# A gated long convolution and a gMLP on one core: the short convolution done with tokens on partitions, its product regrouped inside SBUF

## The chip, the cores and the metric

The kernel runs on one core of a Trainium2 chip. The metric is the device time of one execution in microseconds (us). A core has five engines that run their own instruction lists side by side: TensorE (PE; its weight loads are shown as PEld), VectorE (DVE), ScalarE (ACT), GpSimd (POOL) and SyncE (SP), which here issues nearly all DMA transfers. SBUF is the working memory of 128 partitions, PSUM takes the results of matmuls.

## The reference

There are 2048 tokens of 640 channels. Part A is a short convolution over four tokens, a product with v, a long convolution over all earlier tokens, and a product with the modulated input; part B is a gated MLP whose gate mixes tokens. In short:

```python
mod = silu(c) @ w_mod                       # sa, ca, ga, sb, cb, gb
h = layernorm(x) * (1 + ca) + sa            # x is A_q
k_shift[s] = sum over t of k_pad[s + t] * shift_k[:, 3 - t]
kv = k_shift * v
y = irfft(rfft(kv, 2S) * rfft(ssm_k, 2S))[:S] + kv * ssm_D
x = x + ga * (h * y)
h = layernorm(x) * (1 + cb) + sb
z = gelu(h @ w_in); z1, z2 = halves of z; z2 = layernorm(z2)
out = x + gb * ((z1 * (w_sp @ z2 + b_sp)) @ w_out)
```

## The kernel before

The 640 channels are cut into five tiles of 128 (`u` or `dt` from 0 to 4). The long convolution is a transform by matmuls: a stage one (`stage1`, with the table `F1bd`), a second stage (`forward`, with the table `M2`, 8 items of two frequencies blocks each per tile), the product of the two spectra on VectorE (`product`, L462, tiles `T` or `Tf` with an optional sum `W` on GpSimd or VectorE), the inverse stage (`inv`, table `G2`, result `Z`), a transposing DMA (`zt`, L685) and the last stage (`y`). It is done for the filter (`XK`, `k_item`) and for the signal (`XU`, `u_item`).

Stage one wants the signal in a regrouped form: partition `(g n)`, with `g` one of 8 channels in a group and `n` one of 16 blocks of 128 tokens; along the free axis 16 channel groups `c` by 128 tokens `f` of the block. `ssm_k` is loaded so from DRAM by a rearranged access pattern (`load_X`, L390).

The signal comes from the short convolution. `load_kv` loads k and v of a channel tile by transposing DMAs (L521), so that channels lie on partitions and tokens along the free axis; tile 0 in two halves. `short_conv` makes four diagonal 128x128 matrices `dg` from the four taps. For each of four chunks of 512 tokens, `taps` runs four matmuls with `dg` stationary and k moving, shifted by 0 to 3 tokens, summed in a PSUM tile `sm`; `times_v` (L553) multiplies by v in place. A DMA then writes the product to a DRAM scratch `kv_scr` (`kvw`, L559), and `load_X` reads it back regrouped.

Beside this run the loads of `xt`, the layer norm statistics (`ln1`), the modulation rows from `w_mod` (`wm`), the gating (`gh`), the residual and, as soon as tokens are done, the gMLP: `zz` matmuls with `w_in` (tile `big`) into `pu` and `pz`, gelu on ScalarE, statistics (`stz`) and normalizing on VectorE; then the token mixing by `w_sp` and the output projection, which are written out in program order after the plan (L1013, L1137).

All operations up to the first mixing products are put into a `Plan`: each has the engines that may do it, its reads and writes. A long string `ORDER` gives the order in which they are issued and the engine of each (P, A, D, G, S). Each engine runs its list in that order; SP too, so a DMA whose wait is not yet met holds those behind it. Tiles rotate through a fixed number of buffers by tag, in `SLOTS`. All matmuls of the plan pass through a helper at L245, and copies through one at L248.

Of the kernel before, what the change touches and what calls it, by code (L numbers as in the profile page):

```python
# [10 lines left out]
ALU = mybir.AluOpType  # L11
# [4 lines left out]
P = 128  # L16
# [19 lines left out]
SLOTS = dict(Tf=2, W=2, X=3, X1=4, KH=9, T=3, Z=3, ZT=1, wm=1, big=2, dg=2, st1=2, s1=1, sm=2, pu=2, pz=2)  # L36
# [4 lines left out]
D0 D13 D100 G101 S88 A1 P1032 P7 A4 A10 G5 A23 D15 D102 D109 D103 D110 A112 D115 A111 S2 D6 P1033 P8 A11 D14 A16 D116  # L41
A117 A118 D104 A105 S19 P1034 P26 A106 D90 D121 S82 D86 D17 D122 D18 G119 G113 P1035 P145 A146 P148 D149 S21 S83 D87
P24 A124 A147 D27 D127 S20 A150 P227 A228 A114 P151 A123 A152 P154 A156 P28 D25 S22 A153 D29 D155 P233 A234 G125 A126
P30 S523 D31 D527 P139 D140 G120 S34 P161 A162 P163 S32 G107 P133 P229 G48 A164 S33 P169 A170 D134 D36 S3 P167 A168
A230 G108 P136 D137 P171 A172 P165 A166 P142 A143 G135 D528 P41 A128 D529 D530 D138 P157 A158 P159 A160 S35 G141 P231
A232 D42 S84 S85 P37 D38 P173 P176 A174 A175 D177 P43 D44 A178 P182 D183 P9 A12 G130 P179 A184 P39 D181 D40 A180 P185
D186 S524 A531 A532 P195 D196 P191 D192 S46 S47 P55 D56 A533 P247 A248 G187 G188 P189 S45 P211 D212 G197 G144 G198 P51
D52 A534 P201 D202 D535 P49 D50 G213 P205 G214 A190 S526 A542 P53 D206 P203 A204 G72 S89 P217 D218 G131 A543 P193 P221
D222 P251 A252 D194 P215 A216 A544 G536 D537 P235 P253 P199 D254 D54 A236 P241 A242 G60 S565 P566 G553 P257 A258 S525
D538 D539 S91 G207 G208 P237 P568 A238 P239 A240 P255 A256 G223 P245 D93 A246 P249 A250 S57 G549 G224 D554 G555 P225  # L50
A226 D200 P301 P259 D260 P291 D292 G556 P209 A302 P219 G261 G262 D540 S570 P303 A569 P269 A567 G550 G551 G552 D270
G271 P275 A304 A220 P573 D574 P307 A210 P571 D276 D572 G651 A308 P285 D286 D541 A545 P263 P293 S58 A294 P305 A306 P65
D614 P243 A264 P265 G707 D266 A244 D546 S92 P325 S59 D66 D672 G272 D593 A326 P63 D64 P315 A316 P327 D649 P273 G287
A328 P321 A322 D591 P267 A268 G288 P329 A330 S575 G547 D548 S70 P295 D296 D297 P578 D579 A274 P576 G561 D577 D562 D594
P313 A557 A314 P309 P331 A332 P61 D652 S94 D96 G298 D563 D564 G655 A310 P67 D62 P311 P375 D68 A312 P349 D350 P333 D334
P289 G597 D670 P73 A376 A558 A559 A560 P343 D344 P77 G598 P377 P317 A318 D129 A290 P277 A278 G335 D595 D596 A378 D653
G336 P323 A324 P299 D592 P337 A300 P319 A320 A338 G345 S71 D78 S599 G346 D74 D616 P379 A380 P369 G713 P600 G612 S69
P351 A352 P279 P347 D370 D601 P381 A382 P602 D280 D603 P365 P79 D366 D80 A348 G654 P604 P383 A384 S95 P399 A400 D605
P387 A388 P359 G281 G282 P283 A284 G371 G372 P401 A402 D360 P606 D607 G613 P353 D354 S97 P385 A386 D99 S580 D618 P403
A404 P75 P397 A398 P395 A396 D619 D671 P405 A406 P373 A374 P339 G361 G362 P363 A364 D615 P449 A450 G608 D76 P413 P367  # L60
A368 G355 D340 D414 P407 D408 P341 A342 G617 P453 G709 S620 P621 D622 G674 P393 D650 A454 P389 A394 A390 S81 G356 P623
D624 P451 A452 P439 D440 P357 A358 P625 D626 P391 A392 P455 P427 G409 G410 P627 P417 G609 P581 G673 G656 D428 G429
D430 A456 S98 P411 A412 D418 P471 A472 P473 D628 A474 D634 P431 P457 G419 G420 P443 P479 A458 D444 A480 D629 D632 P467
A468 P421 A432 P423 D424 G445 P475 A476 P433 D434 A582 S657 G639 A422 P415 G676 P461 A462 D631 P477 A478 D630 D638
P463 A464 P658 D659 A416 P465 A466 P441 A442 G446 P660 D635 P481 G435 P447 A448 P497 G710 D661 P662 G436 P437 A438
P425 A426 D482 D663 P664 D498 S583 P517 D518 G677 G483 G484 P485 A486 P507 D508 P499 P459 A460 P469 P501 A470 D665
G675 G519 G520 P521 A522 G509 G510 A500 A132 G708 P487 P584 D502 P513 D488 P511 A512 P491 P489 G503 A490 D514 P515
G504 D492 S678 G668 P505 P679 A516 A506 G493 D494 P495 A585 D633 D680 P681 D682 A496 P719 A720 D636 S586 P683 D684
P715 P721 A722 D716 P685 D686 D687 P717 A718 P587 A588 P723 P726 P725 G666 D691 G711 D689 D688 P724 D727 G714 G692
D728 D729 D758 D730 D759 G760 D690 D731 D732 D734 P735 P1037 D772 P1036 D761 A762 P749 D736 D750 D737 P589 S756 D741  # L70
D740 G763 P764 D766 D767 D768 S757 A590 G667 G610 D696 P765 A769 P742 D733 D738 D693 D834 D771 A770 D637 P794 G773
D695 D836 P812 P784 A795 A813 D751 D754 D774 P818 D837 P791 A775 D739 D694 D835 G697 D698 D776 P778 G838 A819 D839
A785 A840 D842 G843 P777 A782 A783 P787 A788 P816 A817 D780 G712 D841 P814 A815 D640 A792 D779 D781 P808 A809 D796
D752 P822 A823 S844 P820 A821 P824 A825 A846 P798 A848 D743 D789 D702 G669 D703 D706 G845 D744 D745 D746 D900 P801
D611 A799 D644 S1038 P805 A806 D793 P826 A802 A827 D641 D699 D901 D847 G849 P850 A851 D797 P857 P867 A868 D747 P892
A893 D643 D701 D755 D748 P882 D903 S1039 A883 D700 D642 D902 A858 P874 A875 D647 P880 G904 D905 D906 G908 D786 D907
D909 S910 D810 A881 P890 A891 P860 G915 A861 P864 A865 G911 P871 A872 P884 D1054 D1055 D1057 D705 D968 A912 D1056 D807
D811 G913 A885 D648 D704 D753 D645 D966 D646 D967 D969 G970 D866 P888 A889 S1040 D859 D862 D863 P886 A914 P878 A887
A879 P853 D790 D971 D972 G975 D973 A974 A854 D855 D800 P926 P916 A927 S1045 P937 A917 D852 D869 S976 D1046 D803 D804
P933 D918 S1041 A934 P930 P940 A938 D1048 A941 D876 D873 D877 D870 D856 D928 A931 D932 D980 P919 D942 A920 G894 P923  # L80
D921 A924 P948 P958 G979 P952 D895 A959 D922 A949 P946 P954 D977 A896 D925 D929 A947 A953 A955 D939 G978 G981 P982
A983 G828 P999 D1058 D1059 A897 D898 A1000 D943 P985 A986 P989 A990 P992 D829 D830 D831 D1049 A832 D833 D935 D936
D1001 D984 D987 A993 D988 P944 P1006 A945 A1007 P996 A997 D1062 P1003 A1004 D991 P956 G960 D961 D965 A962 A957 D1008
D998 D1002 D1005 D1009 P1020 S1043 A1021 A963 S1042 D994 D995 D899 D1063 P1012 P1014 A1013 P950 G1026 D1027 A1031 A951
D964 D1064 D1066 D1030 A1028 A1015 D1029 D1065 P1024 P1070 A1025 P1072 S1044 P1077 D1067 P1081 D1053 A1073 D1068 D1069
A1071 P1074 D1078 D1082 P1076 D1075 D1079 S1080 P1083 P1018 A1019 P1022 P1010 A1023 D1084 S1085 A1011 D1060 D1061
P1016 A1017 D1047 D1051 D1052 D1050
# [42 lines left out]
def kernel(  # L130
# [43 lines left out]
    dram = ctx.enter_context(tc.tile_pool(name="dram", bufs=1, space=bass.MemoryType.DRAM))  # L174
# [36 lines left out]
    with ExitStack() as pctx:  # L211
# [296 lines left out]
        kv_scr = dram.tile([D, S], BF16)  # L508
        kv_fft = kv_scr.rearrange("(c g) (n f) -> (g n) c f", g=8, f=P)
        SCH = 512  # L510

        def load_kv(dt):
            name = "kv%d" % dt

            n = 2 if dt == 0 else 1

            def load(e, v, h):
                if not v and h == 0:
                    new(name, "big", [P, 2 * S])
                src, o, m = (A_v if v else A_k), v * S, S // n  # L520
                e.dma_start_transpose(tl[name][:, o + h * m:o + (h + 1) * m], src[0, h * m:(h + 1) * m, dt * P:(dt + 1) * P])  # L521
            for v in range(2):
                for h in range(n):
                    ks = [("v", i) if v else ("k", i) for i in range(4 * h // n, 4 * (h + 1) // n)]
                    first = not v and h == 0
                    op("S", "ldk", lambda e, v=v, h=h: load(e, v, h), r=[] if first else [(name, "new")],
                       w=[(name, x) for x in ks] + ([(name, "new")] if first else []), new=[(name, "big")] if first else [], n=n)

        def short_conv(dt):
            name, dg = "kv%d" % dt, "dg%d" % dt  # L530
# [10 lines left out]
            for i in range(S // SCH):  # L541
                ps = "tp%d_%d" % (dt, i)

                def taps(e, i=i, ps=ps):
                    p_ = new(ps, "sm", [P, SCH], F32)
                    for j in range(4):
                        lo = 0 if i else j
                        mm(p_[:, lo:], tl[dg][:, j, :], tl[name][:, i * SCH - j + lo:(i + 1) * SCH - j], j == 0, j == 3)

# [661 lines left out]
```

## Time and profile before

| what | value |
|---|---|
| median of 3 runs | 310.95 us (309.45 to 311.83) |
| the profiled execution | 312.19 us, its span 310.4 us |
| granted TensorE clock | 0.999 |
| busy, share of the span | PE 95%, DVE 82%, ACT 52%, POOL 37% |
| DMA packets | 127953, 45.22 MB |
| queue q1 (hardware) | 68.3% of 16 engines' span |
| HBM | 16.11 MB read, 5.24 MB written |

The span is the time from the first to the last instruction in the profile. A row of a group gives the instructions of one kind, their total busy time and the mean of one in nanoseconds, then the idle time of that engine just before them and what ended it. DMA rows give the number of issues, their size and the median time from issue to landing. In the windows, each engine's busy time in a stretch stands with the number of its instructions, then the granted clock, the DMA share and GB/s. A timeline row gives start and length, both in us. Busy times of matmuls include their passage through the array, so four in a row take less than four times one.

### The profile page before, as it was taken

To read this page: it belongs to the slowest core of one execution; us is meant where nothing else is said; L and a number is where in the kernel's file an instruction comes from. 1 tells how busy PE (TensorE), PEld (TensorE's weight loads), DVE (VectorE), ACT (ScalarE), POOL (GpSimd) and SP (SyncE) were. 2 spreads that over 40 slices of the span, in tenths; PEclk is the share of its full clock that TensorE was granted. 3 is DMA by queue.
4 is the path that set the end of the run, shared out by engine and by line. 5 is a ranking of instruction groups with operands and counts; after the bars stand their busy time and mean duration, and the time that the engine had idled before them with its cause. 6 is when DMAs were issued, how large, how long until landed. Compare 5 with 4: busy or idle time off the path is not lost.

```text
span 310.4 us, 6397 instructions
## 1 busy us (share of the span) xinstructions
PE 295.9 (95%) x2499; PEld 197.3 (64%) x2506; DVE 254.1 (82%) x515; ACT 160.9 (52%) x288; POOL 116.0 (37%) x148
## 2 busy tenths in 40 slices
PE   7897989989999998989999999999999999999996
PEld 2575778867889998645555555455565656555564
DVE  8798998979998988999895998977676858567474
ACT  6987899978888957447666687140101010010100
POOL 2531878838988999555414612000000000000000
PEclk9999999999999999999999999999999999999999
DMA  8999999998995849405698930073938284840414
GB/s 170 216 227 217 257 310 226 207 203 191 221 226 121 193 95 295 143 2 98 123 159 208 185 36 0 2 123 76 201 82 190 63 176 108 131 102 0 104 30 114
DMA packets 127953, 45.22 MB, mean 146 GB/s; under 512 B 117071, under 2 KB 127156, under 8 KB 127924
## 3 DMA queue, kind: packets, MB, share of 16 engines
q1 hardware_dynamic: 127770, 44.78, 68.3%
q8 instruction: 19, 0.31, 0.4%
q14 instruction: 10, 0.08, 0.1%
q10 hardware_dynamic: 154, 0.05, 0.1%
HBM read 16.11 MB, written 5.24 MB: 69 GB/s over the span
## 4 chain that ended last, share of the span: by engine, by line
PE 37%; DVE 19%; POOL 2%; DMA 2%; issue 1%; ACT 1%; POOLq 1%; DVEq 0%; SPq 0%
PE ps L1013 23%; PE po L1137 10%; DVE stz L926 4%; DVE st L704 3%; DMA Z<-Z 2%; PE pz L1013 1%; DVE Tf L462 1%; PE pu L245 1%; DVE xt L698 1%; DVE X L943 1%; POOL rstd L191 1%; DVE T L998 1%; DVE T L462 1%; DVE mv L829 1%; DVE gh L746 1%
## 5 line engine op out<-in xcount | busy, mean ns | idle before, releaser
L245 PEld LDWEIGHTS <-Z 128*128 128x128 bf16 x320 | 31.2, 98 | 28.0 <-DVE Z L871 1.3
L245 PE MATMUL pu<-X,M 128*128 128x128 bf16 (+1 forms) x480 | 45.7, 237 | 2.5 <-DVE Tf L462 2.1
L245 PEld LDWEIGHTS <-M 128*128 128x128 bf16 x480 | 37.3, 98 | 8.7 <-issue 3.1
L1019 ACT COPY m<-ps 128x432 f32<-128x432 f32 x7 | 3.6, 518 | 72.7 <-PE ps L1013 72.7
L1013 PEld LDWEIGHTS <-S 128*128 128x128 bf16 x256 | 25.0, 98 | 22.9 <-issue 1.3
L476 POOL TENSOR_TENSOR W<-Tf 128x256 bf16<-128x256 f32 x47 | 34.7, 760 | 11.4 <-DVE Tf L462 8.1
L245 PE MATMUL pz<-big,Z 128*128 128x432 bf16 x160 | 33.1, 346 | 0.8 <-DVE Z L871 0.8
L248 ACT CAST X<-s 128x1024 bf16<-128x1024 f32 x31 | 31.9, 1030 | 3.1 <-PE s L245 2.9
L1137 PE MATMUL po<-w_o,uT 128*128 128x320 bf16 (+2 forms) x231 | 32.7, 295 | 0.0
L245 PE MATMUL pu<-big,Z 128*128 128x432 bf16 x160 | 32.5, 346 | 0.0
L462 DVE TENSOR_TENSOR Tf<-pu,KH 128x1024 f32<-128x1024 f32 x25 | 30.3, 1219 | 2.6 <-POOL gh L608 1.1
L1013 PEld LDWEIGHTS <-wT 128*128 128x128 bf16 x192 | 18.7, 98 | 15.2
L1137 PEld LDWEIGHTS <-uT 128*128 128x128 bf16 (+1 forms) x231 | 22.2, 98 | 9.7
L245 PEld LDWEIGHTS <-G 128*128 128x128 bf16 x330 | 24.7, 98 | 2.3 <-issue 0.5
L248 ACT CAST KH<-pu 128x512 bf16<-128x512 f32 x40 | 23.0, 600 | 5.9 <-PE pu L245 5.8
L248 ACT CAST Z<-pz 128x512 bf16<-128x512 f32 x38 | 22.3, 602 | 5.3 <-PE pz L245 5.1
L1013 PE MATMUL ps<-T,S 128*128 128x432 bf16 x112 | 22.7, 346 | 0.0
L1013 PE MATMUL ps<-X,wT 128*128 128x432 bf16 x112 | 22.7, 346 | 0.0
L245 PEld LDWEIGHTS <-X 128*128 128x128 bf16 x288 | 18.1, 97 | 6.4 <-DMA X<-kv_scr 1.6
L1013 PE MATMUL ps<-X,S 128*128 128x432 bf16 x112 | 21.6, 346 | 0.0
L245 PE MATMUL s<-F1bd,X 128*128 128x256 bf16 x128 | 19.2, 272 | 1.5 <-DVE X L400 1.2
L245 PE MATMUL sm<-big,dg 128*128 128x512 bf16 (+3 forms) x73 | 19.9, 379 | 0.5
(181 smaller groups left out, 542.6 us busy)
## 6 DMA issues: line engine op xcount, KB each, us to landing
wm<-in_w_mod_dram SPq DMA_DIRECT2D x6, 800.0 KB, 6.2
xt<-in_A_q_dram SPq DMA_DIRECT2D x4, 640.0 KB, 6.2
out_dram<-ot SPq DMA_DIRECT2D x15, 160.0 KB, 2.1
big<-in_B_w_in_dram SPq DMA_DIRECT2D x2, 1080.0 KB, 9.5
X<-in_A_ssm_k_dram SPq DMA_DIRECT2D x4, 512.0 KB, 5.2
kv_scr<-big SPq DMA_DIRECT2D x4, 512.0 KB, 3.5
X<-kv_scr SPq DMA_DIRECT2D x4, 512.0 KB, 4.7
w_o<-in_B_w_out_dram SPq DMA_DIRECT2D x6, 160.0 KB, 3.1
```

The lines of the kernel that those rows point to most:

```text
L191: nc.gpsimd.tensor_tensor(dst, dst, mhalf[:, 0:dst.shape[1]], op=ALU.pow)
L245: nc.tensor.matmul(o, lhsT=w, rhs=x, start=start, stop=stop)
L248: (e.copy if e is nc.scalar else e.tensor_copy)(dst, src)
L462: e.tensor_tensor(T_[:], (tl[pu] if src is None else tl[src])[:, :, :, None, :].to_broadcast(shape), tl[KH][:, :, None, :, :].to_broadcast ...
L476: e.tensor_tensor(tl[W][:, :, o, :], T_[:, :, 0, o, :], T_[:, :, 1, 1 - o, :], op=ALU.add if o else ALU.subtract)
L698: op("GD" if u < NU - 1 else "D", "res", lambda e: e.tensor_tensor(sl, sl, gl, op=ALU.add), r=[("gh", (u, g))], w=[("xt", (u, n)) for n in ...
L704: op("D", "ln2", lambda e, n=n: e.bn_stats(out=st2[:, n, (0, 0, 0, 1, 2)[u], :], in_=xt[:, n, us[0] * DU:(u + 1) * DU]), r=[("xt", (v, n)) ...
L746: op("D", "yml", lambda e, ghv=ghv, py=py, i0=i0, k=k: e.tensor_tensor(ghv, ghv, tl[py][:, i0:i0 + k], op=ALU.mult), r=[py], w=[("gh", (u, ...
L926: op("D", "stz", lambda e, i=i, n=n, fc=fc: e.bn_stats(out=stz[:, n, fc, :], in_=tl[z2][:, i, fc * FC:(fc + 1) * FC]), r=[(z2, (i, fc))], ...
L1013: nc.tensor.matmul(ps[:, :FC], lhsT=lhs[:, s_, :], rhs=rhs(s_), start=(s_ == 0 and not more), stop=(s_ == HT - 1), skip_group_check=more)
L1019: nc.scalar.copy(part[p, m][:], part[p, BANK[m]][:, :FC])
L1137: nc.tensor.matmul(ps[:, :hi - lo], lhsT=uTs[t][:fsz[ft], ft, :], rhs=w_o[:fsz[ft], ft, lo:hi], start=(ft == 0), stop=(ft == NFT - 1))
```

## The change

The roles in the short convolution are turned. k is still loaded by a transposing DMA, now behind 16 columns of zeros (a memset, `kpad`). v is loaded plainly, tokens on partitions. In `taps`, each block of 128 tokens of k, shifted by 0 to 3, is the stationary operand and the diagonal matrix the moving one, so that the result has tokens on partitions: sixteen matmuls of 128 columns for each of the four chunks. `times_v` multiplies by v and writes into a new tile `kvn` with its columns in the order channel group, `g`, `n`, that is with a step of 16 elements. One DMA transpose from SBUF to SBUF (`kx`, for tile 0 in two halves) then brings it into the form that stage one wants. Each half of tile 0 needs all four products of the tile. The DRAM scratch is gone, with its writes and reads.

`SLOTS` has X=4 (was 3), KH=7 (was 9), T=2 (was 3); `kvn` uses the tag X as well. `ORDER` is a new string: beside the changed operations, others stand in another order, and some are done by another engine (for example, up to the first modulation of the gMLP VectorE has two more copies after stage one and five more sums `W`).

```diff
-SLOTS = dict(Tf=2, W=2, X=3, X1=4, KH=9, T=3, Z=3, ZT=1, wm=1, big=2, dg=2, st1=2, s1=1, sm=2, pu=2, pz=2)
+SLOTS = dict(Tf=2, W=2, X=4, X1=4, KH=7, T=2, Z=3, ZT=1, wm=1, big=2, dg=2, st1=2, s1=1, sm=2, pu=2, pz=2)
...
-        kv_scr = dram.tile([D, S], BF16)
-        kv_fft = kv_scr.rearrange("(c g) (n f) -> (g n) c f", g=8, f=P)
-        SCH = 512
+        KO = 16
+        VO = KO + S
...
-                src, o, m = (A_v if v else A_k), v * S, S // n
-                e.dma_start_transpose(tl[name][:, o + h * m:o + (h + 1) * m], src[0, h * m:(h + 1) * m, dt * P:(dt + 1) * P])
+                m, ds = S // n, slice(dt * P, (dt + 1) * P)
+                if v:
+                    e.dma_start(tl[name][:, VO + h * m:VO + (h + 1) * m].rearrange("p (n d) -> p n d", d=P),
+                                A_v[0, h * m:(h + 1) * m, ds].rearrange("(n p) d -> p n d", p=P))
+                else:
+                    e.dma_start_transpose(tl[name][:, KO + h * m:KO + (h + 1) * m], A_k[0, h * m:(h + 1) * m, ds])
...
+            op("GD", "kpad", lambda e: e.memset(tl[name][:, 0:KO], 0.0), r=[(name, "new")], w=[(name, "pad")])
...
                 def taps(e, i=i, ps=ps):
-                    p_ = new(ps, "sm", [P, SCH], F32)
-                    for j in range(4):
-                        lo = 0 if i else j
-                        mm(p_[:, lo:], tl[dg][:, j, :], tl[name][:, i * SCH - j + lo:(i + 1) * SCH - j], j == 0, j == 3)
+                    p_ = new(ps, "sm", [P, 4, P], F32)
+                    for a in range(4):
+                        o = KO + (4 * i + a) * P
+                        for j in range(4):
+                            mm(p_[:, a, :], tl[name][:, o - j:o - j + P], tl[dg][:, j, :], j == 0, j == 3)
...
                 def times_v(e, i=i, ps=ps):
-                    o = S + i * SCH
-                    vsl = tl[name][:, o:o + SCH]
-                    e.tensor_tensor(vsl, tl[ps][:], vsl, op=ALU.mult)
+                    if i == 0:
+                        new(kv, "X", [P, DU // 8, P])
+                    o = VO + 4 * i * P
+                    e.tensor_tensor(tl[kv][:].rearrange("p c (g n) -> p n (c g)", n=NCB)[:, 4 * i:4 * i + 4, :], tl[ps][:],
+                                    tl[name][:, o:o + 4 * P].rearrange("p (a d) -> p a d", d=P), op=ALU.mult)
...
-                op("S", "kvw", lambda e, sl=sl: e.dma_start(kv_scr[dt * P:(dt + 1) * P, sl],
-                                                                   tl[name][:, S + sl.start:S + sl.stop]),
-                   r=[(name, ("v", i)) for i in range(4 * h // n, 4 * (h + 1) // n)], w=[("kvs", (dt, h))], n=n)
+                def regroup(e, h=h):
+                    if h == 0:
+                        new(X, "X", [P, DU // 8, P])
+                    cs = slice(h * DU // 8 // n, (h + 1) * DU // 8 // n)
+                    e.dma_start_transpose(tl[X][:, cs, :], tl[kv][:, cs, :].rearrange("p c x -> p (c x)"))
+                op("S", "kx", regroup, r=[(kv, i) for i in range(4)] + ([(X, "new")] if h else []),
+                   w=[(X, h)] + ([] if h else [(X, "new")]), new=[] if h else [(X, "X")], n=n)
...
-            load_X("XU%d" % u, kv_fft, u, [("kvs", (u, h)) for h in range(2 if u == 0 else 1)])
```

## The prediction

> **What bounds the kernel now.** I read the windows of ten microseconds first, to see which engine has no slack in which stage.
>
> ```profile
> core 0: us, PE busy (x) PEld busy (x) DVE busy (x) ACT busy (x) POOL busy (x), PEclk, DMA share, GB/s
> 20.00:30.00 10.00, 7.88 (x64) 5.10 (x63) 8.39 (x17) 8.28 (x18) 0.63 (x3) 1.00 1.07 221
> 60.00:70.00 10.00, 8.75 (x89) 6.84 (x88) 7.93 (x20) 7.60 (x11) 4.36 (x5) 1.00 1.28 186
> 90.00:100.00 10.00, 10.00 (x166) 9.44 (x165) 9.04 (x11) 8.03 (x14) 9.53 (x10) 1.00 0.73 183
> 140.00:150.00 10.00, 10.00 (x56) 5.28 (x54) 9.60 (x31) 7.98 (x16) 5.03 (x6) 1.00 0.70 126
> 206.00:310.00 104.00, 101.55 (x620) 60.02 (x618) 68.52 (x122) 7.97 (x14) 0.00 (x0) 1.00 0.52 108
> ```
>
> Three stages. From about 134 us on, TensorE is full: 10.00 of 10 in the gMLP products, 101.55 of 104 in the mixing. What comes before, the long convolution, is shared: VectorE, ScalarE and TensorE all stand at 8 to 10, and DMA at 1.0 or more until 75 us. So the change, which lies before 90 us, pays or costs by one number: when the gMLP products can begin. They begin at 133.6 us (first matmul into `pz` from `big`), right behind VectorE's first modulation of `Z` at 133.14. The chain of waits, whose pieces show from 110 us, is almost all VectorE until 195 us. In the page's slices VectorE's row says the same of the early part: some idle at the start, then nearly none.
>
> Next the rows that price the touched work, by form and by DMA issue:
>
> ```profile
> L245 PE MATMUL sm<-big,dg 128*128 128x512 bf16 x58 | 16.8, 380 | 0.5
> L370 PE MATMUL sm<-ident,M 128*128 128x128 bf16 x32 | 2.4, 219 | 0.7 <-DVE big L553 0.7
> L553 DVE TENSOR_TENSOR big<-sm,big 128x512 bf16<-128x512 f32 x20 | 13.5, 686 | 2.4 <-DMA big<-in_A_v_dram 1.4 <-PE pz L245 0.5 <-PE sm L245 0.4
> ...
> kv_scr<-big SPq DMA_DIRECT2D x4, 512.0 KB, 3.5
> X<-kv_scr SPq DMA_DIRECT2D x4, 512.0 KB, 4.7
> uT<-u SPq DMA_TRANSPOSE x16, 2.9
> big<-in_A_v_dram SPq DMA_TRANSPOSE x6, 5.6
> ZT<-Z SPq DMA_TRANSPOSE x4, 8.3
> ```
>
> Last the timeline, for the places where the old route is late:
>
> ```profile
> 15.20 0.97 SPq L559 DMA_DIRECT2D kv_scr<-big  x2
> 16.66 3.40 SPq L521 DMA_TRANSPOSE big<-in_A_v_dram  x1
> 20.34 1.00 SPq L390 DMA_DIRECT2D X<-kv_scr  x2
> ...
> 23.77 0.39 PE L245 MATMUL pz<-F1bd,X 128*128 128x256 bf16 x2 [1.15 <-DMA X<-kv_scr]
> ...
> 68.19 0.23 DVE L400 TENSOR_TENSOR X<-X,D_col 128x16 bf16<-128x16 bf16 x1 [2.03 <-DMA X<-in_A_ssm_k_dram]
> ```
>
> The product of the first channel tile leaves at 15.20, is read back only at 20.34 (its issue stands behind a 3.40 us transposing issue on SP) and lands at 23.77. The second gap, 2.03 us at 68, is a plain load behind the transposes of the last tile.
>
> **The change part by part.**
>
> *Taps on TensorE.* 80 matmuls of 512 columns become 320 of 128, each with its own weight load. Four of 512 take 1.03 us in the timeline, so (1.03 - 0.38)/3 = 0.217 each, 17.4 us in all. Eight flips of 128 columns, each with a load, take 0.61, so (0.61 - 0.22)/7 = 0.056 each: 320 make 17.9. I take +0.6, of which half falls where TensorE is full: +0.3. Upper bound, no load hidden: a load is 98 ns, so 320 x 98 = 31 us more; the flip row, the same size with a load each, excludes nearly all of it, and I keep +8 (320 x 25 ns) as an upper end. Below zero: the columns to stream are the same, which excludes a gain.
>
> The Trainium skill (TensorE: Matmul & The Clock Gate, section Back-to-back issue gap) says that a sustained stream of load and matmul pairs costs some 81 ns at 128 columns and 131 at 512. By it the taps would go from 10.5 to 25.9 us, +15.4, against this change; the flips here run at 56 ns, and four of 512 at 217, so the rows decide.
>
> *The product on VectorE.* Still 20 of 128x512, but written with a step of 16 elements instead of in a row. The nearest row is `gh<-gh,sm` (L678): same size, read from PSUM, written in runs of four elements with gaps, 683 ns against 686. I take 0. The far row: adding `D_col` to one element of every 128 (L400) takes 198 ns at its shortest for 8 and 231 for 16, 4 ns an element against some 1.1 here; 20 x 512 x 3 ns = 30 us. It is a small instruction, so mostly overhead; that end stays for a rival.
>
> The Trainium skill (SBUF — State Buffer, section Door 1: The DMA port swizzle, its note on cachelines) holds that strides past 16 bytes pay a penalty, and gives no figure; no run shows it yet.
>
> *The pad.* Five memsets of 16 columns, 0.1 us each by the 0.10 us memset of `mpi`, four on POOL, which has slack: 0.
>
> *DMA and SP.* Out go the transposing loads of v, the writes to DRAM and the reads back; their SP issues add up to 17.2 + 2.9 + 2.6 = 22.7 us. In come six plain loads of v (0.5 us issue each as `X<-in_A_ssm_k_dram`, 3.1) and six transposes within SBUF. By size between `uT` (224 KB: 1.23 issue, 2.9 to landing) and `ZT` (1 MB: 4.9 and 8.3) a whole one takes 2.55 and 4.6, a half 1.35 and 3.1: 12.9 us of issue. SP gets 6.7 us freer, and 2.5 MB of writes vanish from DMA engines that are full until 75 us.
>
> But the regroup is issued by SP in order, and it waits for all four products of its tile. In the new order the first one stands ahead of the second load of `xt` and of k of tile 1, which before was issued at 10.37. It can go at about 15.0 (the four products need what they needed, 15.44), lands 1.35 + 3.1 later, 19.5 instead of 23.77. So the first convolved product, 28.39 now, could start some 4 us sooner. ScalarE and VectorE must still copy stage one; I take 24.7. K of tile 1 then goes at 18.3 and lands near 24.5, its v at 26 to 28 (5.2 to land). VectorE's next instruction after the first product is the product of tile 1, ready at 25.8: a wait of 0 to 2.5. I take 0.5.
>
> *The order of everything else is new too,* and this is the biggest term. Counting both programs' VectorE lists up to the first modulation and pricing each by its row: two more stage-one copies (+2.4), five more sums `W` (+2.2, taken from POOL), one more set of statistics (+1.1), one more copy `ZT` (+0.7), less `yml`, `xn`, `diag` and others (-2.6): 130.8 becomes 134.6. Up to the first convolved product it is 26.9 before and 24.4 after, because four products of v moved behind it. So from there to the modulation 103.9 becomes 110.2. Now that stretch takes 133.14 - 28.39 = 104.75, a ratio of 1.008. After: 24.7 + 110.2 x 1.008 = 135.8, +2.7. ScalarE's list loses 9 us in the same stretch, so some waits on it go. After the modulation, to the last of the sums `T`, VectorE gets about 4 more (69.8 against 66.0 by rows); it has 7 us idle there now and TensorE eight fillers instead of six behind the last z2, so 0, with +2 if that cover is gone.
>
> *Buffers.* X four instead of three, KH seven instead of nine, T two instead of three. Waits of the products on KH are 0.7 us in all now. With seven the eighth K item of a tile must wait for a product; the new order puts it there. 0, at most one copy and one forward per tile, 5 x 1.0.
>
> *Sum.* +2.7 (VectorE), +0.5 (tile 1), +0.3 (taps), -1.5 (the 2.03 gap mostly gone with less on DMA): +2.0. The profiled execution took 312.19, its span 310.4; the median is 1.24 below that. 310.95 + 2.0 = 313.0.
>
> **The rivals.**
>
> *Faster: idle time pays.* By the windows VectorE is idle 12.9 us before 133.6. If the extra work falls into that idle time, since ScalarE is 9 us lighter and DMA no longer full, then the stretch stays at 104.75: 24.7 + 104.75 - 2.0 = 127.5, less 5.7; with a fifth of that lost, 306.4. For it: the gaps at 20 to 30 and 60 to 70 both end on a DMA. Against: later than 70 us VectorE has only some 4 us idle.
>
> *Slower: SP held by the regroup.* Each regroup waits in order with loads behind it. If k and v of tile 1 land after 28 and tile 2 follows as late, the wait is 2.5 twice and the 1.5 is not won: 310.95 + 2.0 + (5.0 - 0.5) + 1.5 = 319. It decides from the point where v of tile 1 lands over 2 us after the first product ends (25.8). For it: 4.7 us issues of k while DMA is full. Against: SP is 6.7 us freer.
>
> *Slower: the scattered write or the loads.* One more pass for the product, 20 x 0.53 = 10.6, or loads at 25 ns each, 8: 310.95 + 2 + 8 to 10.6 = 322.
>
> **How the numbers follow.** Forecast 0.45, faster 0.25, SP held 0.20, write or loads 0.10. A change of 1% (3.1 us) is about what a measurement of this kernel tells from none. The forecast's own range is 310 to 316 (half the extra vector work absorbed, or the tile 1 wait in full): of its 0.45, 0.31 lie within 1%, 0.14 slower. Faster gives 0.22 and 0.03 within; the two others 0.30, all slower but 0.02 of it. So faster 0.22, same 0.36, slower 0.42. Range 305.5 to 320: below it and beyond it the rest of the faster rival and the third.
>
> **What would show it.** Right: `X` of tile 0 landing near 19.5, the first `Tf` or `T` near 24.7, the product still 686 ns, sixteen taps in about 1.05 us, no 2 us gap near 68, first zz matmul near 135. Wrong: the product over 0.8 us; taps over 1.3 us for sixteen; VectorE waiting on `big` near 26 for over 2 us; zz starting before 131 (idle absorbed it) or the loss coming after 190, where I put none.

## The result and the profile after

The changed kernel takes 346.66 us (median of 4 runs, 345.4 to 347.95) against 311.23 (4 runs, 309.45 to 311.83): a ratio of 1.115, 95% interval 1.108 to 1.122, that is 35.4 us slower. The profiled execution took 347.78 us, its span 345.5, the granted clock 0.974 in the mean (0.999 before).

First the windows of the changed kernel, with the columns of those shown of before: the stretch and its length, busy us and number of instructions of each engine, the granted clock (PEclk), the DMA share and GB/s.

```profile
core 0: us, PE busy (x) PEld busy (x) DVE busy (x) ACT busy (x) POOL busy (x), PEclk, DMA share, GB/s
20.00:30.00 10.00, 7.61 (x84) 6.04 (x83) 9.77 (x24) 7.61 (x14) 2.10 (x3) 1.00 0.52 117
40.00:50.00 10.00, 8.87 (x106) 8.04 (x104) 9.97 (x9) 4.44 (x9) 2.45 (x3) 0.78 0.51 105
90.00:100.00 10.00, 6.96 (x70) 5.99 (x70) 8.54 (x10) 3.73 (x8) 7.24 (x9) 0.83 0.65 99
241.00:345.00 104.00, 101.79 (x622) 60.10 (x619) 67.95 (x121) 8.20 (x15) 0.00 (x0) 1.00 0.53 108
```

Before, the window from 40 to 50 us read:

```profile
40.00:50.00 10.00, 9.66 (x110) 8.42 (x108) 8.86 (x17) 9.48 (x17) 6.89 (x9) 1.00 1.02 288
```

In the first two rows of the changed kernel VectorE is nearly full and the others have slack: from 40 to 50 us it is busy 9.97 of 10 with nine instructions, where before it made seventeen in 8.86; ScalarE stands at 4.44 (9.48 before), GpSimd at 2.45. From 90 to 100, where before TensorE stood at 10.00, it now stands at 6.96, and its granted clock at 0.83. The last row, the mixing, is as before (101.55 of 104 there). So the loss lies ahead of the gMLP. The first gMLP matmul starts at 167.06 us instead of 133.59: 33.5 later. The stretch from there to the mixing is 73.4 us (71.7 before), the rest the same within 0.5. The whole stretch up to the first gMLP matmul, before and after:

```profile
0.00:133.60 133.60, 123.36 (x1491) 99.56 (x1498) 120.99 (x227) 108.05 (x192) 92.61 (x118) 1.00 0.92 204
0.00:167.10 167.10, 133.44 (x1738) 113.97 (x1738) 156.68 (x234) 100.95 (x180) 94.08 (x123) 0.96 0.71 148
```

VectorE is busy 156.68 of 167.10 us, 35.7 more than before in a stretch 33.5 longer. TensorE is busy 10.1 us more, at a granted clock of 0.96 instead of 1.00, but stands idle for 33.7 us of the stretch, where it was idle for 10.2 before: the lower clock is not what fills it.

Next the groups of the touched work (line, engine, operation, tiles and shapes, count; busy us in all, mean ns of one; idle time before it and what ended that), then the DMA issues (median us to landing last):

```profile
L244 PE MATMUL sm<-dg,big 128*128 128x128 bf16 x320 | 22.6, 229 | 10.6 <-DVE X L558 9.5 <-DVE gca_bf L658 0.7 <-DMA big<-in_A_k_dram 0.5
L558 DVE TENSOR_TENSOR X<-sm,big 128x512 bf16<-128x512 f32 x20 | 45.9, 2388 | 4.1 <-DMA big<-in_A_v_dram 3.7
```

```profile
big<-in_A_v_dram SPq DMA_DIRECT2D x4, 512.0 KB, 6.3
big<-in_A_k_dram SPq DMA_TRANSPOSE x6, 6.6
X<-X SPq DMA_TRANSPOSE x6, 5.3
```

The second line holds the case: the product has the same count, shape and operands as L553 before, and 2388 ns where that had 686. Its 45.9 us against 13.5 are 32.4 us more on VectorE. TensorE now waits for that tile: 9.5 us ahead of the taps alone. The timeline shows how this spreads:

```profile
13.95 4.50 DVE L558 TENSOR_TENSOR X<-sm,big 128x512 bf16<-128x512 f32 x2
18.87 4.50 DVE L558 TENSOR_TENSOR X<-sm,big 128x512 bf16<-128x512 f32 x2
23.39 2.64 SPq L569 DMA_TRANSPOSE X<-X  x2
32.14 1.21 DVE L461 TENSOR_TENSOR Tf<-pu,KH 128x1024 f32<-128x1024 f32 x1
37.07 4.47 DVE L558 TENSOR_TENSOR X<-sm,big 128x512 bf16<-128x512 f32 x2 [3.72 <-DMA big<-in_A_v_dram]
```

The four products of tile 0 take VectorE from 13.95 to 23.3. Only then can SyncE issue the regrouping, at 23.39, and all the loads behind it in its queue; v of tile 1 is late by that, and VectorE, held up itself, waits another 3.72 us for it at 37. In the chain that ended last, by line, the product is now VectorE's largest piece, with 8% of the span (before it is not in that line, but the chain of before shows only pieces from 110 us on, so the two do not compare):

```profile
PE ps L1022 21%; PE po L1146 9%; DVE X L558 8%; PE pu L244 5%; DVE Tf L461 5%; PE pz L244 4%; DVE stz L935 4%; DVE T L461 3%; DMA ZT<-Z 3%; PE s L244 2%; DVE st L714 2%; DMA big<-in_A_v_dram 2%; PE sm L244 2%; DVE xt L708 2%; PE pz L1022 1%
```

### The profile page after: what moved, and what is told of

Its sections match the earlier page's. It is cut to its first block, busy times and chain, and to the rows that moved or that the text cites. A ratio compares the mean times of both kernels' runs of the same rounds, so it can differ in the third digit from the quotient of the medians.

```text
span 345.5 us, 6896 instructions
## 1 busy us (share of the span) xinstructions
PE 307.5 (89%) x2746; PEld 211.8 (61%) x2746; DVE 292.7 (85%) x528; ACT 154.9 (45%) x277; POOL 116.1 (34%) x150
## 4 chain that ended last, share of the span: by engine, by line
PE 45%; DVE 39%; issue 5%; DMA 5%; SPq 2%; POOL 2%; ACT 1%; DVEq 0%; POOLq 0%; ACTq 0%
PE ps L1022 21%; PE po L1146 9%; DVE X L558 8%; PE pu L244 5%; DVE Tf L461 5%; PE pz L244 4%; DVE stz L935 4%; DVE T L461 3%; DMA ZT<-Z 3%; PE s L244 2%; DVE st L714 2%; DMA big<-in_A_v_dram 2%; PE sm L244 2%; DVE xt L708 2%; PE pz L1022 1%
## 5 line engine op out<-in xcount | busy, mean ns | idle before, releaser
L244 PE MATMUL pu<-X,M 128*128 128x128 bf16 (+1 forms) x480 | 47.9, 242 | 6.4 <-DVE Tf L461 4.9
L558 DVE TENSOR_TENSOR X<-sm,big 128x512 bf16<-128x512 f32 x20 | 45.9, 2388 | 4.1 <-DMA big<-in_A_v_dram 3.7
L244 PEld LDWEIGHTS <-M 128*128 128x128 bf16 x480 | 38.4, 100 | 11.5 <-issue 7.0
L475 POOL TENSOR_TENSOR W<-Tf 128x256 bf16<-128x256 f32 x42 | 30.9, 754 | 27.8 <-DVE Tf L461 24.2
L247 ACT CAST X<-s 128x1024 bf16<-128x1024 f32 x29 | 29.6, 1020 | 13.0 <-PE s L244 13.0
L244 PE MATMUL pu<-big,Z 128*128 128x432 bf16 x160 | 34.2, 358 | 1.1 <-ACT M L929 0.6
L244 PE MATMUL pz<-big,Z 128*128 128x432 bf16 x160 | 32.3, 346 | 0.2 <-ACT M L929 0.2
L244 PE MATMUL sm<-dg,big 128*128 128x128 bf16 x320 | 22.6, 229 | 10.6 <-DVE X L558 9.5
L244 PEld LDWEIGHTS <-big 128*128 128x128 bf16 x320 | 20.6, 103 | 12.0 <-issue 11.3
L244 PEld LDWEIGHTS <-G 128*128 128x128 bf16 x330 | 25.6, 101 | 3.7 <-issue 1.1
```

The costliest lines, as they stand in the source:

```text
L244: nc.tensor.matmul(o, lhsT=w, rhs=x, start=start, stop=stop)
L247: (e.copy if e is nc.scalar else e.tensor_copy)(dst, src)
L475: e.tensor_tensor(tl[W][:, :, o, :], T_[:, :, 0, o, :], T_[:, :, 1, 1 - o, :], op=ALU.add if o else ALU.subtract)
L558: e.tensor_tensor(tl[kv][:].rearrange("p c (g n) -> p n (c g)", n=NCB)[:, 4 * i:4 * i + 4, :], tl[ps][:], tl[name][:, o:o + 4 * P].rearran ...
```

## The experiments

The kernel before was run beside them on the same chips, with medians of 310.32, 310.19 and 309.98 us. Each ratio below is to the median beside it.

**The step of the write, one for each tile.** The edit, shortened:

```diff
+s = (16, 8, 4, 2, 1)[dt]        # elements from one written element to the next
+w_ = kvn[:] viewed as "p (h d s) -> p h s d"
-e.tensor_tensor(kvn[:] as "p n (c g)" [:, 4i:4i+4, :], ps, v)
+e.tensor_tensor(w_, ps, v)
```

> The changed kernel with another step of the product's write for each channel tile: 16, 8, 4, 2 and 1 elements of 2 bytes (32, 16, 8, 4, 2 bytes), all inside the same tile kvn; sizes, sources and order are unchanged. The regrouped signal of tiles 1 to 4 is in another order of channels and tokens, so those results are other ones. Theory W (the price is the write's step): tile 0 stays at 2.36 us an instruction as in the changed kernel, tile 4 is 0.69 as before the change, and those between tell whether the price comes with every jump or from a jump size on. Rival R (the price is in the sources: v read from the new place, PSUM read in another form): all twenty stay at 2.3 to 2.4. If the price comes only where the next element is 32 bytes away, tiles 1 to 4 are all 0.69 and the time falls by 16 x 1.7 = 27 us to 319; if it grows with the step, tile 1 lies between, near 1.3 to 2.4. By the Trainium skill (SBUF - State Buffer, the note on 16-byte cachelines), a line holds 8 bf16, so tiles 0 and 1 would pay and tiles 2 to 4 would not.

330.34 us (one run). VectorE's timeline, start and length first, x2 meaning two instructions in a row; tiles 0 to 4 from top to bottom, that is steps of 32, 16, 8, 4 and 2 bytes:

```profile
14.48 4.50 DVE L562 TENSOR_TENSOR X<-sm,big 128x512 bf16<-128x512 f32 x2
41.44 4.70 DVE L562 TENSOR_TENSOR X<-sm,big 128x512 bf16<-128x512 f32 x2
56.55 1.31 DVE L562 TENSOR_TENSOR X<-sm,big 128x512 bf16<-128x512 f32 x1
76.98 0.73 DVE L564 TENSOR_TENSOR X<-sm,big 128x512 bf16<-128x512 f32 x1
93.13 0.68 DVE L564 TENSOR_TENSOR X<-sm,big 128x512 bf16<-128x512 f32 x1
```

So 2.25, 2.35 (halves of the pairs), 1.31, 0.73 and 0.68 us for the same 512 elements. The shapes and sources are the same, and in the changed kernel, where all tiles write in steps of 32 bytes, none of the twenty products is under 2.298 us; so the step makes the price, and the tile does not. From 16 bytes on it is paid in full, some 4.5 ns an element, and does not grow further.

**The product in a row.** Everything else as in the changed kernel; the regrouping of the columns is left out.

```diff
-e.tensor_tensor(tl[kv][:].rearrange("p c (g n) -> p n (c g)", n=NCB)[:, 4 * i:4 * i + 4, :], ...
+e.tensor_tensor(tl[kv][:, 4 * i:4 * i + 4, :], ...
```

> The changed kernel with the product written in a row (unit step); the transpose then brings it in another order, which leaves the regrouping out. Theory W: the product falls from 2.39 us to 0.69, 20 x 1.70 = 34 us of VectorE work go, the gMLP products start at 133 to 136 instead of 166.8, and the time is 310 to 315. Rival S (the SP queue held behind the regroup, and the new order of work, cost most; the slow product only fills VectorE's waits): the product falls to 0.69 but the time stays above 328, with X of tile 0 still late and k of tile 1 issued after 20 us.

317.28 us (316.5 to 317.8), ratio to before 1.021 (1.015 to 1.027); first gMLP matmul at 138.45. The product:

```profile
L558 DVE TENSOR_TENSOR X<-sm,big 128x512 bf16<-128x512 f32 x20 | 13.3, 683 | 1.7 <-PE sm L244 1.7
```

The step of the write is 346.66 - 317.28 = 29.4 us. What is left of the change still costs 317.28 - 310.32 = 7.0 by the kernel before that ran beside it; so neither theory was right about the time (310 to 315, or above 328).

**The whole result by runs of eight.** If the partitions go `(n g)` in place of `(g n)`, eight channels of one block lie side by side; the signal then needs a stage-one table of its own.

```diff
-tl[kv][:].rearrange("p c (g n) -> p n (c g)", n=NCB)[:, 4 * i:4 * i + 4, :]
+tl[kv][:].rearrange("p c (n g) -> p n c g", n=NCB)[:, 4 * i:4 * i + 4]
```

> The changed kernel with the signal's partitions ordered block, channel instead of channel, block: the product is then written in runs of eight elements (16 bytes) with 256 bytes between runs, and stage one of the signal has a table of its own (some 1.5 us more of small instructions at the start). It computes the whole result. Theory W: the product takes 0.69 to 0.8 us, the time is that of the row version plus 0 to 2: 310 to 316. If a jump of any kind costs (one in eight elements), the product is near 0.9 and the time 3 to 5 us longer. Rival S: above 328.

317.22 us (316.94 to 317.55), ratio 1.021 (1.015 to 1.027), product 683 ns. So the regrouping need not cost VectorE's product anything: runs of 16 bytes go at the price of a row. The time is above the 310 to 316 that was expected, by the same 7 us as the row kernel's.

**VectorE's time by itself.** The kernel before, with its product in place done three times.

```diff
-e.tensor_tensor(vsl, tl[ps][:], vsl, op=ALU.mult)
+for _ in range(3): e.tensor_tensor(vsl, tl[ps][:], vsl, op=ALU.mult)
```

> The kernel before with the product by v done three times over in place (so its result is another one): 40 more instructions of VectorE, 0.62 us each back to back, 25 us between 10 and 90 us, and nothing else changed. Theory W says that VectorE's time in this stage is the kernel's time one to one, so the kernel gets 21 to 26 us longer (332 to 337). Rival S: the idle time of VectorE (12.9 us before 133.6) and a freer order take half of it: 8 to 14 us (319 to 325).

334.31 us (332.82 to 334.8), ratio 1.075 (1.068 to 1.083). Its group of products:

```profile
L554 DVE TENSOR_TENSOR big<-sm,big 128x512 bf16<-128x512 f32 x60 | 40.9, 688 | 1.4
```

40.9 - 13.5 = 27.4 us of work added to VectorE, and 24.0 us to the kernel: 0.88 for one. By that rate the 32.4 us of the changed kernel are worth 28.4; the row kernel says 29.4. So VectorE's added time is enough to explain the write's share, to within 1 us.

**Before's order, buffers and start.** Taps, plain v, pad and SBUF transfer as in the change; the product in a row over v (regrouping left out); 3, 9 and 3 buffers of X, KH and T, and before's `ORDER`, with the transfer where the write to DRAM stood.

> The changed kernel's taps, plain v, pad and SBUF transfer, but the product written in a row in place over v as before (the regrouping by columns left out, so the transfer moves the rows), X, KH and T with 3, 9 and 3 buffers as before, and the written-out order of before; the transfer stands where the write to DRAM stood. What is left of the change with the wide step gone cost 6.9 us (317.2 against 310.3). Theory O (those 6.9 us are the new order with its late start and the smaller KH and T): 309 to 311.5, first gMLP matmul near 133, product 0.68 us. Rival C (they are the new work itself: tap pairs, the queue held by the transfer, its traffic): 315 to 318, first gMLP matmul at 136 to 138. A value between shares them out.

312.13 us (10 runs, 311.15 to 313.23), ratio 1.007 (1.004 to 1.009). Five of the seven us are the order or the buffers; the 309 to 311.5 of the first theory is missed by 0.6. Two windows of its profile, the long convolution and the first gMLP stage:

```profile
0.00:133.30 133.30, 124.01 (x1737) 109.81 (x1737) 121.46 (x227) 107.31 (x192) 92.92 (x123) 1.00 0.88 185
133.30:205.00 71.70, 70.29 (x387) 37.31 (x388) 63.97 (x166) 44.43 (x81) 23.25 (x31) 1.00 0.47 92
```

These are before's stages to within 0.3 us (133.6 and 71.7). The 1.9 us by which its median is above before's can't be placed in them: the profiled execution of before had a span of 310.4, its 13 runs beside this one 306.7 to 309.4. Some 0.45 of the 1.9 lie outside the span: the time less the span is 2.20 to 2.30 us in its ten runs and 1.75 to 1.84 in before's. Where the other 1.5 lie stays open.

**After's order with before's buffers.** The kernel in a row, in place over v, with 3, 9 and 3 buffers.

> The written-out order of after, with the product in a row in place over v (the regrouping by columns left out, as in the row kernel), so that no tile is needed for it and X, KH and T have 3, 9 and 3 buffers again. It differs from the row kernel (317.28) by the buffers alone, and from the kernel in before's order (312.13) by the order alone. Theory N (the order costs, the buffers do not): 316.5 to 317.8. Rival B (the two KH and one T that were given up cost): 312 to 315.

317.5 us (316.45 to 317.77), ratio 1.024 (1.020 to 1.027): against the 317.28 of the row kernel the buffers cost nothing that shows, and the order costs 317.5 - 312.13 = 5.4. The same two stages of its profile:

```profile
0.00:136.70 136.70, 125.24 (x1738) 109.58 (x1738) 127.12 (x234) 99.83 (x180) 94.40 (x123) 1.00 0.91 181
136.70:210.20 73.50, 71.88 (x392) 37.49 (x389) 67.55 (x174) 45.66 (x83) 21.77 (x28) 0.98 0.46 91
```

VectorE has 127.12 us of work in the first stage instead of 121.46 (seven instructions more, ScalarE twelve fewer), and 67.55 instead of 63.97 in the second. The stages are 3.4 and 1.8 us longer. In the second, which TensorE nearly fills, its own busy time is 71.88 instead of 70.29, at a granted clock of 0.98; no run tells whether that or VectorE's work makes the 1.8.

**Before's start only.** The row kernel with the 82 operations up to the last product of tile 0 in before's order.

> The kernel with the product in a row (317.28), its order changed at the start alone: the 82 operations up to the last product of tile 0 stand in the order of before, the rest in the order of after. Before's VectorE made its first eviction at 9.16 us and the row kernel at 12.91, with TensorE's first matmul at 1.65 and 2.68. Theory S (the late start is carried to the end, since VectorE is over 90% busy after it): 313 to 315, first gMLP matmul near 135. Rival (the start is caught up by 60 us and the loss lies later): 316.5 to 318, first gMLP matmul near 138.

316.49 us (316.08 to 317.0), ratio 1.020 (1.017 to 1.024): 0.8 us of the 5.4, within reach of the noise. The late start is mostly caught up.

**The transfer without its wait.** The row kernel, with the transfer reading the k half.

```diff
-e.dma_start_transpose(tl[X][:, cs, :], tl[kv][:, cs, :] ...)       # waits for four products
+e.dma_start_transpose(tl[X][:, cs, :], tl[name][:, KO + ... ])       # k, loaded long before
```

> The kernel with the product in a row (317.28), with the transfer reading the k half of the tile, which is there long before, in place of the product: the same 512 KB moved, but SyncE's queue is no longer held until VectorE has made the product (13.2, 11.5, 10.7, 8.0 and 3.9 us in the changed kernel). Theory Q (holding the queue costs part of the 6.9 us): 313 to 315.5. Rival (held, but nothing behind it is needed sooner): 316.5 to 318.

314.75 us (314.26 to 315.52), ratio 1.015 (1.011 to 1.018): 2.5 us less. TensorE's wait for X before the stage one of tile 1, 1.33 us at 40.86 in the row kernel, is gone (that stage one starts at 39.91). But this kernel both frees the queue and lets X land early, so it doesn't say which of the two is worth it.

**Loads ahead of the transfers.** The kernel by runs of eight, with seven loads moved ahead on SyncE's queue.

> The kernel that writes runs of eight (317.22, the whole result), with seven loads moved ahead of the transfers that they stood behind on SyncE's queue: the second part of x, k and v of tile 1 ahead of the transfers of tile 0; c, the third block of w_mod and the third part of x ahead of that of tile 1; v of tile 3 ahead of that of tile 2. Theory Q (the queue held by a transfer that waits for VectorE costs some 2.5 us, as the kernel with the product's wait taken away gave 314.75 against 317.28): 314.5 to 316. Rival (that gain came from X landing earlier, not from the loads behind): 316.8 to 317.8.

320.3 us (319.29 to 322.18), ratio 1.032 (1.028 to 1.036): 3.1 slower, where one theory had 2 faster. TensorE's timeline shows why. First the kernel by runs of eight, then this one, at the stage one of tile 1:

```profile
41.28 0.61 PE L244 MATMUL s<-F1bd,X 128*128 128x256 bf16 x4 [1.65 <-DMA X<-X]
```

```profile
43.34 1.03 PE L244 MATMUL s<-F1bd,X 128*128 128x256 bf16 x4 [3.69 <-DMA X<-X]
```

With the loads ahead, the transfer of tile 1 goes out at 33.88 and takes 5.90 us to issue (33.55 and 4.03 without), and X is what TensorE waits for. So having those loads sooner gained less than the later X cost. The theory of the held queue falls in this form; that the 2.5 us of the run before are X's earlier landing is the reading that fits both, though no run changed that alone.

**Blocks innermost.** The loops of the product turned, so that it writes runs of four.

> The changed kernel with the loop order of the product turned: the four token blocks innermost, so that each instruction writes 128 runs of four elements (8 bytes, 32 bytes from run to run) and reads PSUM and v with steps of 512 and 256 bytes between neighbours; the whole result is computed. Theory of lines (one price for each 16 bytes entered by consecutive writes, about 4.4 ns): 128 runs, so 0.7 us by the plain pass, 317 us. Rival E (every element pays where neighbours in the address are not in one burst, or strided reads pay as strided writes do): 2.3 us, 346 us.

320.77 us (one run), the product 1043 ns: neither 0.7 nor 2.3. The next run takes the two halves of it apart.

**Forms of reading and writing.** The edit in words:

```diff
+tile 0: row <- turn(ps), turn(v)      tile 1: row <- turn(ps), v      tile 2: row <- ps, turn(v)
+tile 3: runs of four, 32 bytes apart <- ps, v      tile 4: pairs, 16 bytes apart <- ps, v
```

> One form of the product for each tile, the values not in their places: tile 0 writes a row and reads PSUM and v turned (512 and 256 bytes between neighbours); tile 1 reads PSUM alone turned; tile 2 reads v alone turned; tile 3 reads in a row and writes runs of four, 32 bytes apart; tile 4 reads in a row and writes pairs, 16 bytes apart. The kernel with token blocks innermost took 1.04 us for a product (20.4 us in all), turned reads and runs of four together. Theory L (4.4 ns for each 16-byte piece that a write enters, reads free): tiles 0 to 2 0.68, tile 3 0.7, tile 4 1.1 to 1.2 us. Rival R (turned reads cost): tile 0 1.04, tile 3 0.68, and tiles 1 and 2 tell which read. Rival F (a run that fills half of its 16 bytes costs): tile 3 1.04, tiles 0 to 2 0.68.

318.65 us (one run). The groups by form, in the order of tiles 0 to 4:

```profile
L563 DVE TENSOR_TENSOR X<-sm,big 128x512 bf16<-128x512 f32 x4 | 4.0, 1039 | 0.0
...
L565 DVE TENSOR_TENSOR X<-sm,big 128x512 bf16<-128x512 f32 x4 | 2.6, 683 | 0.9 <-PE pu L244 0.9
...
L567 DVE TENSOR_TENSOR X<-sm,big 128x512 bf16<-128x512 f32 x4 | 4.0, 1031 | 0.0
...
L569 DVE TENSOR_TENSOR X<-sm,big 128x512 bf16<-128x512 f32 x4 | 2.7, 680 | 0.0
...
L572 DVE TENSOR_TENSOR X<-sm,big 128x512 bf16<-128x512 f32 x4 | 2.7, 684 | 0.4 <-PE sm L244 0.4
```

The turned read of v from SBUF costs 0.35 us, that of PSUM nothing. Runs of four are free, and pairs too: 4.4 ns for each 16-byte piece entered would have made them 1.1 us, so that theory falls as well. The price falls on single elements of two bytes, 8 bytes or more apart.

**The write on other engines.** The product in a row on VectorE, then a copy that makes the 32-byte steps. The edit, shortened:

```diff
+e.tensor_tensor(vsl, ps, vsl)
+(nc.scalar, nc.scalar, nc.gpsimd, nc.gpsimd, e)[dt] copies vsl to kvn in steps of 16 elements
```

> The product in a row in place on VectorE, and a copy of its own that writes it in steps of 32 bytes (the whole result is computed, with 20 instructions more): on ScalarE for tiles 0 and 1, on GpSimd for 2 and 3, on VectorE for 4. Rows of before: ScalarE writes 128x512 from PSUM in 0.58, GpSimd a bf16 128x512 in 0.6 to 1.2, VectorE 0.68 for the product. Theory L2 (the price belongs to the memory's 16-byte pieces, so every engine pays it): 2.2 to 2.5 us on each engine. Rival V (it belongs to VectorE): ScalarE 0.55 to 0.7, GpSimd 0.6 to 1.2, VectorE 2.3 us.

361.51 us (one run).

```profile
L564 POOL COPY X<-big 128x512 bf16<-128x512 bf16 x8 | 19.0, 2397 | 5.5 <-DVE big L559 5.5
L562 ACT COPY X<-big 128x512 bf16<-128x512 bf16 x8 | 17.9, 2542 | 3.1 <-DVE big L559 3.1
L566 DVE COPY X<-big 128x512 bf16<-128x512 bf16 x4 | 6.3, 1564 | 0.1
```

GpSimd takes 19.0 / 8 = 2.4 us, ScalarE 17.9 / 8 = 2.2 (its mean is 2.54, since its instructions overlap), VectorE's copy 1.56. In rows, ScalarE wrote 128x512 from PSUM in 0.58 and GpSimd a bf16 128x512 in 0.6 to 1.2. All pay, VectorE's plain copy the least; moving the scatter to another engine does not escape it. Neither theory fits whole: the price is not VectorE's alone, and VectorE's copy is below what both gave it.

No run beat the kernel before. The nearest, in before's order, stood at 312.13 without the regrouping, so taking the trip to DRAM away gained nothing there: the first convolved product starts at 27.82 instead of 28.39. In that kernel VectorE waits 1.57 us, up to 23.32, for v of tile 1, whose load stands behind the transfer in SyncE's queue (there was no such wait before), so what a transfer that holds nothing up would gain is not shown.

## Why the prediction was wrong, point by point

**The product: the step that failed.** I took 0, by "the nearest row", `gh<-gh,sm` (L678), which writes runs of four. That row was priced rightly (runs of four: 680 ns) and was the wrong row: the change writes elements one by one, and the far row, adding `D_col` to one element in 128, was the only one I had priced that did. It gave 4 ns an element and 30 us in all; the runs showed 2388 / 512 = 4.7 ns and 34 us of instruction time. I had worked it out and set it aside as "a small instruction, so mostly overhead". But the 4 ns was the slope between 8 and 16 elements, from which overhead cancels. And the rival that was to hold that end was priced at one more pass (10.6 us), not at the 30 just computed, so the range left it out. The bounds were right; the choice between them was by size and operands, where it should have been by the form of the write.

The Trainium skill (SBUF — State Buffer, section Door 1: The DMA port swizzle, note on cachelines) asks for at least two hits in a 16-byte line. The pairs (two hits, 684 ns) and the single elements at 16 and 32 bytes (one hit, 2.35 and 2.25 us) agree with it; steps of 8 bytes also hit each line twice and took 1.31, where a row takes 0.68, which it does not explain. The note spoke against this change, and I weighed it as a sentence without a figure, where the `D_col` row had the figure.

**VectorE bounds the stage: right.** 0.88 us of kernel time for each added us of VectorE (the product done three times), 29.4 for 32.4 in the change. For the 5.7 us that the new order adds to VectorE it was 3.4, so the rate is not the same for all added work. The rival by which idle time absorbs extra work nearly whole falls with this. (I gave that idle time as 12.9 us; the windows make it 133.60 - 120.99 = 12.6.)

**Taps: right.** TensorE's busy time in the stage is 124.01 against 123.36 with before's order, +0.65, where I had +0.6; but the trace of before holds only 73 of its 80 tap matmuls, so this agreement is good to some 1.5 us (7 x 0.217). Sixteen taps took 1.05 us where nothing held them, as forecast.

The Trainium skill's 81 ns for a load and matmul pair of 128 columns (TensorE: Matmul & The Clock Gate, section Back-to-back issue gap) is not seen here: with the 0.22 us that one matmul takes alone, (1.05 - 0.22) / 15 = 55 ns.

**DMA and SP: the moment of issue right, the gain wrong.** With the product in a row the regrouping went at 15.41 (forecast 15.0); in the changed kernel at 23.39, by the write alone. But the two issues took 4.73 us rather than 2.7, and the first convolved product started at 27.72, not 24.7. It was not X that held it: TensorE began stage one of tile 0 at 21.86, right behind its work on the filter and without a wait for X. I had also taken 2.5 us of VectorE's work out of this stretch (26.9 to 24.4 by rows); the trace has 23.69 us busy before and 23.24 in the row kernel. Those 3 us are most of what the row kernel (317.28) lost on the forecast (313.0). The 2.03 us gap at 68 did go. (The line between `uT` and `ZT` gives 4.8 us to landing for a whole transfer, not 4.6; the median measured is 5.3.)

**The new order's lists: right behind the first convolved product.** From there to the first modulation I had 110.2 x 1.008 = 111.1 us; the row kernel took 137.62 - 27.72 = 109.9, with 6.2 us more of VectorE (103.06 against 96.84) where I had 6.3. **Buffers: right**, nothing that shows. **After the modulation** I took 0, with +2 if the cover was gone: it was 1.8 (73.5 against 71.7) in after's order with before's buffers and 0.4 in the row kernel (71.9 against 71.5, from the first gMLP matmul to the last into `pz`); whether the cover went is not shown.

**SP held by the regroup.** Its signs showed (v of tile 1 late, a 3.72 us wait), but as a consequence of the write. In the row kernel a transfer that need not wait is worth 2.5 us; in the kernel by runs of eight, putting loads ahead of it costs 3.1.

## What to carry to other kernels

Price a write by its inner run: before a layout change is moved from a DMA to a compute engine, look for the row in the profile that writes the same run length in the same element size, however small the instruction, and take the slope between two of its sizes. See whether the permutation can be turned so that runs of two or more elements come out: here changing the order of the partitions and one table made a 2388 ns product 683. And where an engine is busy for some 90% of a stage, count most of its added time (0.6 to 0.9 of it here) and compare that with all that a removed transfer could give.

## What the runs showed of the hardware

Writing 128x512 two-byte elements on VectorE, from a product: in a row 0.68 us; pairs 16 bytes apart 0.68; runs of four 0.68; single elements 4, 8, 16 and 32 bytes apart 0.73, 1.31, 2.35 and 2.25. Reading the SBUF operand in steps of 256 bytes: 1.03; reading PSUM in steps of 512 bytes: 0.68, no cost. A copy of such a tile in SBUF to 32-byte steps: ScalarE 2.2 us, GpSimd 2.4, VectorE 1.56. The granted clock from 40 to 50 us was 0.78 in the changed kernel, 0.83 in the row kernel and 0.66 with the loads ahead, and 1.00 in before, in before's order and in the kernel by runs of eight. TensorE had waited there or just ahead of it in the three with the lower clock, but also, for 1.65 us, in the last one, so the runs do not show what lowers it.
